# Output products in column tiles of two feature blocks by two token halves, in a float32 convolution and SwiGLU kernel

## The chip, the cores and the metric

The kernel runs on one core of a Trainium2 chip. A core has five engines that work side by side: TensorE (PE in the profile, its weight loads PEld), VectorE (DVE), ScalarE (ACT), GpSimd (POOL) and SyncE (SP), which here only issues DMAs. The metric is the device time of one execution in microseconds (us), less is better. Before the change it was 2796.47 us, the median of three runs (2788.88 to 2798.66).

## The reference

Two blocks follow each other: a causal convolution of 7 taps, whose taps differ by head, and a feed-forward block with a norm and a gated unit. Everything is float32.

```python
# x: (8, 4096, 192), weight: (8 heads, 7 taps)
w = softmax(weight, axis=-1)
x_pad = concatenate([zeros(8, 6, 192), x], axis=1)
x_unf = x_pad[:, arange(4096)[:, None] + arange(7)[None, :], :]   # seven shifted copies
y = einsum('hk,bskhg->bshg', w, x_unf).reshape(32768, 192)

rms = sqrt(mean(y * y, axis=-1, keepdims=True) + 1e-6)
xn = y / rms * rms_g
g, val = xn @ w_gate, xn @ w_val              # 192 -> 1536, twice
out = (silu(g) * val) @ w_out                 # 1536 -> 192
```

## The kernel before

The 32768 tokens are worked through in 32 pairs of token tiles, 2 x 512 tokens each. The first pair is computed plainly, by code of its own, beside the preparation of the weights. Each of the other 31 goes through two stages on TensorE, here called P and O:

- P, the up-projection. Both projections are computed as sums of 15 products for each of four groups of hidden features, in two halves of the array: 120 matmuls of 64 rows by 512 columns. They read `xb` (the normalised input, features by tokens) and `xc` (sums of parts of it, the "input sums").
- O, the output products. The product with `w_out` is done by seven products of half-size blocks (Strassen's scheme in Winograd's form), each over six chunks of 128 hidden features.

Each `yield` in a generator of matmuls is one step. A list, ORDER, tells how the steps and all other operations follow each other in a pair: `p2` is two steps of matmuls, `VX5` is input sum 5 on VectorE, `AS40.1.0` a copy on ScalarE, `GS3.1` a sum on GpSimd; a minus sign at the end means that the operation belongs to the pair before. Its beginning and its end:

```python
ORDER = (
    "p2 VT22- AS40.1.0 VT11- p2 AS40.0.0 Dload- Vbc- p2 AF0.0.0 VC.0.0 Dst1- AF0.1.0",
    ...
    "p1 Asq p2 GX1 GS4.5 p3 VC22 p2 GS4.4 p2 Vred p6 VC21 p2 VX5 p4 VX10 p3 VX9 VT21 p2",
    "Gpow p4 VT12 p3 GX4 p3",
)
```

The steps of a pair:

```python
def products(self):
    for u in self.units:                       # P: four groups of hidden features
        for v, i in CHAIN:                     # 15 products
            for h in range(2):                 # two halves of the array's rows
                u.product(h, v, i)             # 64 x 512 columns
                yield
    for form, b, lo, hi in OUTS:               # O: seven forms, 42 chunks in all
        first = form in (1, 7)
        if first:
            self.open(b, False)
        for k in range(lo, hi):
            cols = self.left(form, k).rearrange("p (b q e) -> p q b e", q=NQ, e=Q)
            for m in range(NM):                # NM = 3 blocks of Q = 32 output features
                for q in range(NQ):            # NQ = 4 quarters of the tokens
                    nc.tensor.matmul(
                        out=self.bank(b)[q * Q : (q + 1) * Q, m * P : (m + 1) * P],
                        lhsT=RIGHT[form][:, k, m, :], rhs=cols[:, q],
                        start=(first and k == 0 and m == 0), stop=True,
                        skip_group_check=True, tile_position=(0, q * Q),
                    )
                yield
```

The stationary operand is a block of the weights, 128 hidden features by 32 output features; it fills one column tile of the array, 32 of its 128 columns. The hidden values stream through it, 128 tokens in one matmul. Four such matmuls, one for each column tile, belong together.

The results stand in a PSUM bank with output features in the partitions and tokens along the columns. VectorE turns blocks of 32 x 32 into the output tile:

```python
def turn(self, src, g, n):
    if g not in self.o_sb:
        self.o_sb[g] = outs.tile([P, T // P, D], F32, name="o_sb")
    to = self.o_sb[g][:].rearrange("p b (m n e) -> p m n b e", n=2, e=Q)
    for m in range(NM):
        nc.vector.transpose(
            out=to[:, m, n],
            in_=src[:, m * P : (m + 1) * P].rearrange("p (b e) -> p b e", e=Q),
        )
```

During O the engines other than TensorE already work for later pairs: the convolution of the pair after next (`cv`, and `sq`, `red`, `pow` for the norm), and the input sums of the next pair (`X`), after its input has been fetched:

```python
def fetch(p):                                  # Dfetch: four DMAs of 384 KB
    xd = scr.pop(p)
    for g in (1, 0):
        for rows in (LOW, UPP):
            nc.sync.dma_start(
                out=xb[rows, g],
                in_=xd[:, g * T : (g + 1) * T].rearrange("(k p) t -> p k t", p=HP),
            )

def x_sum(i, eng="V"):                         # VX0 .. VX10, or GX
    d, a, b = XSUM[i]
    e = nc.gpsimd if eng == "G" else nc.vector
    e.tensor_tensor(out=xc[:, d, :], in0=x_op(a), in1=x_op(b), op=ALU.add)
```

`xb` and `xc` exist once, so the fetch waits for the last product of P that reads them.

Of the kernel before, what the change touches and what calls it, by code (L numbers as in the profile page):

```python
# [19 lines left out]
def kernel(  # L20
# [10 lines left out]
    nc = tc.nc  # L31
    P = nc.NUM_PARTITIONS
# [10 lines left out]
    T = 512  # L43
# [3 lines left out]
    HP = P // 2  # L47
    KP = D // HP
    Q = 32
    NQ = P // Q  # L50
# [7 lines left out]
    LOW, UPP = slice(0, HP), slice(HP, P)  # L58
# [29 lines left out]

    SPAN = 1509
    ORDER = (  # L90
        "p2 VT22- AS40.1.0 VT11- p2 AS40.0.0 Dload- Vbc- p2 AF0.0.0 VC.0.0 Dst1- AF0.1.0",
        "Dst0- p2 Gmul- p2 AS41.1.0 VC.1.0 AS41.0.0 p2 AS00.1.0 VS00.0.0 p2 GX7- VD5.0.0 p2",
        "VD5.1.0 AS42.0.0 VS42.1.0 p2 Dplace- VR1.0.0 AS51.1.0 AS51.0.0 p2 VR1.1.0 p2 AF2.0.0",
        "VR0.1.0 p1 VR0.0.0 AF2.1.0 p1 AF3.0.0 p1 VF3.1.0 AS44.0.0 p1 AS44.1.0 AG1.0.0",
        "VR5.0.0 p2 GM1.1.0 AG5.0.0 VR2.0.0 VR2.1.0 p2 VR3.1.0 AG4.0.0 p3 VR5.1.0 AS40.0.1 p1",
        "VR3.0.0 AS40.1.1 GM5.1.0 p1 VM4.1.0 AF0.0.1 AG3.0.0 p2 AF0.1.1 p1 VC.0.1 AG0.0.0 p1",
        "VC.1.1 GM3.1.0 p1 AS41.1.1 VS41.0.1 p1 GM0.1.0 GS3.0 VS00.0.1 p1 AS00.1.1 p2 VD5.0.1",
        "p1 VD5.1.1 p1 AS42.0.1 AS51.0.1 VS51.1.1 p1 GS1.0 VR1.0.1 AS42.1.1 p1 AG2.0.0 p1",
        "VR1.1.1 p1 VR0.0.1 p1 AF2.0.1 VR0.1.1 GM2.1.0 p1 AF2.1.1 p1 VF3.0.1 p1 AF3.1.1",
        "VS44.0.1 p1 AG0.0.1 GS3.1 p1 VR2.0.1 p1 GS2.0 AS44.1.1 AG1.0.1 p2 VR2.1.1 AG2.0.1",  # L100
        "GM1.1.1 p1 VR5.0.1 p1 AG4.0.1 VR5.1.1 p1 GM2.1.1 VM4.1.1 p1 AG5.0.1 AS40.0.2 p1",
        "VR3.0.1 VR3.1.1 p2 AS40.1.2 AF0.0.2 GM0.1.1 p1 AF0.1.2 VC.0.2 GS3.2 p1 VC.1.2 p1",
        "AS41.0.2 AS41.1.2 p1 GM5.1.1 p1 AS00.0.2 p2 GS1.2 VS00.1.2 p1 VD5.0.2 AS51.0.2 p1",
        "VD5.1.2 AS42.0.2 p1 AS51.1.2 p1 GS2.2 VS42.1.2 p1 AG3.0.1 VR1.0.2 p1 GM3.1.1 p1",
        "VR0.1.2 p1 AF2.0.2 VR0.0.2 p1 AF2.1.2 p1 AF3.0.2 p1 GS4.2 AS44.0.2 p1 VR1.1.2 p1",
        "GS1.1 VF3.1.2 AG0.0.2 p1 AS44.1.2 p1 VR5.0.2 VR2.0.2 p1 VR2.1.2 AG1.0.2 AG5.0.2 p1",
        "VR3.1.2 p1 GM1.1.2 AG4.0.2 VR5.1.2 AS40.0.3 p2 GM0.1.2 GM5.1.2 VR3.0.2 p1 AS40.1.3",
        "p1 VM4.1.2 p1 AF0.0.3 p1 AF0.1.3 AG3.0.2 p1 VC.0.3 p1 VC.1.3 p1 VS41.0.3 GM3.1.2",
        "AS41.1.3 AS00.0.3 p2 VS00.1.3 AG2.0.2 p1 GS3.3 GS1.3 p2 VD5.1.3 AS42.0.3 AS51.1.3",
        "VD5.0.3 VS42.1.3 p2 AS51.0.3 VR1.0.3 GS2.1 p1 GM2.1.2 p2 VR0.1.3 VR1.1.3 p1 GS2.3 p1",  # L110
        "AF2.0.3 AF2.1.3 p1 VR0.0.3 p1 VF3.1.3 p1 AF3.0.3 VS44.0.3 p1 AG1.0.3 p1 VS44.1.3",
        "AG0.0.3 VR5.0.3 p3 GM1.1.3 VR3.0.3 GS3.4 VR2.0.3 p1 GS4.3 Acv0_2 p1 VR3.1.3 p1",
        "Vcv1_2 p2 AG4.0.3 p1 AG3.0.3 p1 GM3.1.3 p1 Dfetch VM4.1.3 Acv0_1 p3 Acv0_0 p2",
        "AG2.0.3 p2 Vcv1_0 p1 VR5.1.3 p1 GS1.4 VR2.1.3 p1 Vcv1_1 p1 GS3.5 p1 Ac1 p1 AG5.0.3",
        "p4 Vcv2_2 p2 GS2.4 p6 Vcv2_0 p1 VM5.1.3 p3 Vcv2_1 As7 p2 Vcv3_2 p1 Vcv3_0 p1 GS1.5",
        "p4 Vcv3_1 p1 GS4.1 p1 Vcv4_0 p2 Vcv5_0 GS2.5 p3 GS4.0 Vcv4_2 p5 Vcv4_1 p1 Vcv5_2 p3",
        "GX0 Vcv5_1 p5 VX3 Ac2 Vcv6_2 p3 VX2 p7 VX8 p4 GM2.1.3 Vcv6_0 VX6 VM0.1.3 p9 Vcv6_1",
        "p1 Asq p2 GX1 GS4.5 p3 VC22 p2 GS4.4 p2 Vred p6 VC21 p2 VX5 p4 VX10 p3 VX9 VT21 p2",
        "Gpow p4 VT12 p3 GX4 p3",
    )  # L120

    cst = ctx.enter_context(tc.tile_pool(name="cst", bufs=1))
# [115 lines left out]
    def load_out(i):  # L238
# [28 lines left out]
        out=taps[:], in0=w_sb[:], in1=stat[:].to_broadcast([P, H, K]), op=ALU.subtract  # L267
# [7 lines left out]
        out=taps[:], in0=taps[:], in1=ssum[:].to_broadcast([P, H, K]), op=ALU.mult  # L275
# [403 lines left out]
    def put(at, do):  # L679
        heapq.heappush(line, (at, next(tick), do))  # L680
# [10 lines left out]
    def copy(eng, dst, src, s=1):  # L691
        if eng == "A":
            nc.scalar.activation(out=dst, in_=src, func=AF.Copy, scale=float(s))  # L693
        elif s < 0:
            nc.vector.tensor_scalar(out=dst, in0=src, scalar1=-1.0, scalar2=None, op0=ALU.mult)
        else:
            nc.vector.tensor_copy(out=dst, in_=src)
# [86 lines left out]
    NM = D // (2 * Q)  # L784
# [16 lines left out]
    RIGHT = {1: B11, 2: B21, 3: B22, 4: T4, 5: T1, 6: T2, 7: T3}  # L801

    class Pair:
# [35 lines left out]
        def products(self):  # L839
            for u in self.units:  # L840
                for v, i in CHAIN:
                    for h in range(2):
                        u.product(h, v, i)
                        yield
            for form, b, lo, hi in OUTS:
                first = form in (1, 7)
                if first:
                    self.open(b, False)
                for k in range(lo, hi):
                    cols = self.left(form, k).rearrange("p (b q e) -> p q b e", q=NQ, e=Q)  # L850
                    for m in range(NM):
                        for q in range(NQ):
                            nc.tensor.matmul(  # L853
                                out=self.bank(b)[q * Q : (q + 1) * Q, m * P : (m + 1) * P],
                                lhsT=RIGHT[form][:, k, m, :], rhs=cols[:, q],
                                start=(first and k == 0 and m == 0), stop=True,
                                skip_group_check=True, tile_position=(0, q * Q),
                            )
                        yield

        def some(self, b):
            return self.bank(b)[:, 0 : NM * P]
# [1 line left out]
        def turn(self, src, g, n):  # L864
            if g not in self.o_sb:
                self.o_sb[g] = outs.tile([P, T // P, D], F32, name="o_sb")
            to = self.o_sb[g][:].rearrange("p b (m n e) -> p m n b e", n=2, e=Q)
            for m in range(NM):
                nc.vector.transpose(  # L869
                    out=to[:, m, n],  # L870
                    in_=src[:, m * P : (m + 1) * P].rearrange("p (b e) -> p b e", e=Q),
                )

        def sum(self, form, k, eng):
# [9 lines left out]
        def do(self, eng, name):  # L884
            act, *at = name.split(".")
            p, n = self.p, NM * P
            if len(at) == 2:
                self.units[int(at[1])].do(eng, act, int(at[0]))
            elif at:
                self.sum(int(act[1]), int(at[0]), eng)  # L890
            elif act == "c1":
                self.open("Y", True)
                copy(eng, self.some("Y"), self.some("X"))
            elif act in ("s7", "c2"):
                t = self.tl[act] = tiles.pop(0)
                copy(eng, t[:, 0:n], self.some("Z" if act == "s7" else "X"))
            elif act in ("C22", "C21"):
                t = self.tl["s7" if act == "C22" else "c2"][:, 0:n]
                b = "X" if act == "C22" else "Z"
                nc.vector.tensor_tensor(out=t, in0=self.some(b), in1=t, op=ALU.add)  # L900
                if b == "Z":
                    self.close(b)
            elif act in ("T22", "T21"):
                t = self.tl.pop("s7" if act == "T22" else "c2")
                self.turn(t, 1, int(act[2]) - 1)
                tiles.append(t)
            elif act in ("T11", "T12"):
                b = "Y" if act == "T11" else "X"
                self.turn(self.bank(b), 0, int(act[2]) - 1)
                self.close(b)  # L910
            elif act in ("st0", "st1"):
                g = int(act[2])
                r = p * PT + g * T
                nc.sync.dma_start(
                    out=out[r : r + T, :].rearrange("(j p) d -> p j d", p=P), in_=self.o_sb.pop(g)[:]
                )
            else:
                self.ahead(eng, act)

# [16 lines left out]
    def plain(hts):  # L936
# [27 lines left out]
        def values():  # L964
            for u, g, f in groups:
# [7 lines left out]
                yield  # L973

        return products(), silus(), values()

    LAG = 138
# [116 lines left out]
    p, sl, v = plain(hts)  # L1094
# [31 lines left out]
    c = base + 200  # L1126
# [60 lines left out]
```

## Time and profile before

| | before |
|---|---|
| time, median of three runs | 2796.47 us |
| span of the profiled run | 2787.9 us |
| PE busy, matmul records | 2650.6 us, 39418 |
| DVE busy, instructions | 2400.9 us, 3914 |
| ACT busy, instructions | 1505.7 us, 2778 |
| POOL busy, instructions | 2078.4 us, 1695 |
| mean granted TensorE clock | 0.989 |
| DMA queue q1: packets, MB | 444240, 133.44 |

A line of the profile that describes a group of instructions names the line of the program, the engine, the operation, output and inputs, the shape and the count; behind the bar stand the time in which the group was busy, the mean of one in ns, and the idle time of the engine just before. The timeline has the start and the length in us, then the instructions that it merges; in brackets stands idle time before them, and what ended it. A table of stretches has for each engine its busy time and the number of instructions, then the granted clock, the DMA engines' share and the rate. "issue" is time in which an engine waited for nothing that the profile shows. Each float32 matmul of the program stands as two records in the trace. SP's entries are the issuing of DMAs, not their transfers.

The program's lines that matter: L732 is the product of P, L853 that of O, L655 an input sum, L445 a tap of the convolution, L869 a transpose into the output tile, L646 the fetch of the next pair's input, L882 a sum of hidden values on GpSimd, L693 a copy on ScalarE and L697 one on VectorE.

### The profile page before, as it was taken

The numbers are of one execution on the slowest core, as the hardware profiler recorded it, in microseconds if no ns is written. First come the engines' busy times: TensorE is split into PE (matmuls) and PEld (weight loads), VectorE is DVE, ScalarE is ACT, GpSimd is POOL, SyncE is SP. The second block draws the span as 40 slices with busy tenths as digits, with TensorE's granted clock in tenths as the row PEclk, the third lists the DMA queues.
The fourth block names the chain that finished last, engine by engine and source line by source line (L and its number), as shares of the span: only waits on it lengthen the run. The fifth ranks groups of instructions, "written<-read, shape, count | busy, mean of one in ns | idle before, by whom it ended". The sixth has DMA issues, their size and how long they took to land.

```text
span 2787.9 us, 91977 instructions
## 1 busy us (share of the span) xinstructions
PE 2650.6 (95%) x39418; PEld 1826.5 (66%) x39418; DVE 2400.9 (86%) x3914; ACT 1505.7 (54%) x2778; POOL 2078.4 (75%) x1695
## 2 busy tenths in 40 slices
PE   6999999999999999999999999999999999999999
PEld 3766667666677566676666666666766666666666
DVE  8898888988888988888888888888988888888876
ACT  5266544565445665446655456544566544565444
POOL 3987777777768777677777777777877777877767
PEclk9999999999999999999999999999999999999999
DMA  6311332131231213322223213223212233121210
GB/s 135 65 41 37 60 60 49 35 59 37 60 60 30 54 37 60 60 37 47 45 52 60 56 29 58 38 60 60 41 44 49 47 60 60 25 58 37 47 36 14
DMA packets 445209, 139.34 MB, mean 50 GB/s; under 512 B 385024, under 2 KB 419328, under 8 KB 444673
## 3 DMA queue, kind: packets, MB, share of 16 engines
q1 hardware_dynamic: 444240, 133.44, 24.1%
q8 instruction: 308, 5.05, 0.8%
q14 instruction: 101, 0.83, 0.1%
q10 hardware_dynamic: 560, 0.03, 0.0%
HBM read 83.87 MB, written 49.55 MB: 48 GB/s over the span
## 4 chain that ended last, share of the span: by engine, by line
PE 77%; DVE 9%; issue 6%; POOL 3%; ACT 2%; DMA 1%; SPq 1%; POOLq 0%; DVEq 0%
PE ps L732 56%; PE ps L853 19%; DVE xc L655 3%; DVE ps L445 1%; POOL ht L882 1%; PE ps L990 1%; DVE ht L756 1%; ACT ps L437 1%; PE ps L950 1%; DMA xh<-in_x_dram 1%; POOL nt L882 1%; DVE y L445 1%; DVE s L471 1%; DVE o_sb L869 1%; POOL xc L655 1%
## 5 line engine op out<-in xcount | busy, mean ns | idle before, releaser
L732 PE MATMUL ps<-xc,wf 64*128 64x512 f32 x4960 | 1287.0, 595 | 6.1 <-DVE o_sb L869 4.9
L732 PEld LDWEIGHTS ps<-xc,wf 64*128 64x128 f32 x4960 | 630.0, 186 | 486.2 <-issue 359.6
L732 PE MATMUL ps<-xb,wf 64*128 64x512 f32 x2480 | 739.0, 589 | 0.0
L776 POOL TENSOR_TENSOR ht<-ht,tile 128x512 f32<-128x512 f32 x330 | 418.7, 1276 | 196.0 <-ACT tile L769 177.2
L693 ACT ACTIVATE tile<-ps 128x512 f32<-128x512 f32 (+1 forms) x634 | 360.5, 593 | 348.0 <-PE ps L732 185.8
L693 ACT ACTIVATE tls<-ps 128x512 f32<-128x512 f32 (+1 forms) x513 | 293.0, 588 | 437.5 <-PE ps L853 253.1
L732 PEld LDWEIGHTS ps<-xb,wf 64*128 64x128 f32 x2480 | 329.4, 187 | 252.3 <-issue 240.9
L693 ACT ACTIVATE ps<-ps 128x512 f32<-128x512 f32 (+1 forms) x651 | 358.9, 580 | 141.5 <-PE ps L732 90.4
L776 POOL TENSOR_TENSOR ht<-ht,tls 128x512 f32<-128x512 f32 x228 | 290.5, 1277 | 113.9 <-ACT tls L769 103.5
L882 POOL TENSOR_TENSOR early<-ht 128x512 f32<-128x512 f32 x279 | 354.7, 1276 | 9.7
L853 PE MATMUL ps<-ht,wo_sb 128*32 128x128 f32 x10416 | 338.4, 280 | 14.1 <-issue 13.0
L853 PEld LDWEIGHTS ps<-ht,wo_sb 128*32 128x32 f32 x10416 | 305.7, 113 | 47.5 <-POOL ht L776 23.5
L445 DVE SCALAR_TENSOR_TENSOR ps<-xh,tp,ps 128x512 f32<-128x512 f32 x435 | 299.8, 750 | 16.7 <-ACT ps L437 15.6
L853 PE MATMUL ps<-early,x 128*32 128x128 f32 x6696 | 220.4, 281 | 77.7 <-issue 77.6
L756 DVE TENSOR_TENSOR tile<-ps,tile 128x512 f32<-128x512 f32 x371 | 250.8, 684 | 25.3 <-ACT tile L693 21.8
L882 POOL TENSOR_TENSOR ht<-ht 128x512 f32<-128x512 f32 x186 | 238.2, 1281 | 30.1 <-DVE ht L776 20.4
L853 PE MATMUL ps<-ht,x 128*32 128x128 f32 x8928 | 258.7, 273 | 1.6 <-issue 1.0
L853 PEld LDWEIGHTS ps<-early,x 128*32 128x32 f32 x6696 | 199.0, 113 | 88.1 <-issue 87.0
L853 PEld LDWEIGHTS ps<-ht,x 128*32 128x32 f32 x8928 | 247.1, 110 | 8.1 <-issue 7.8
L769 ACT ACTIVATE tile<-tile 128x512 f32<-128x512 f32 x371 | 230.3, 628 | 0.0
L756 DVE TENSOR_TENSOR ht<-ps,tile 128x512 f32<-128x512 f32 x333 | 222.9, 684 | 4.6
L756 DVE TENSOR_TENSOR ht<-ps,tls 128x512 f32<-128x512 f32 x287 | 194.3, 683 | 2.3
(128 smaller groups left out, 3346.7 us busy)
## 6 DMA issues: line engine op xcount, KB each, us to landing
xb<-xd SPq DMA_DIRECT2D x124, 384.0 KB
out_dram<-o_sb SPq DMA_DIRECT2D x64, 384.0 KB
xd<-yn SPq DMA_DIRECT2D x248, 96.0 KB
xh<-in_x_dram SPq DMA_DIRECT2D x192, 105.0 KB
xh<-in_x_dram SPq DMA_DIRECT2D x56, 98.4 KB
ht<-in_moe_w_gate_dram SPq DMA_DIRECT2D x12, 192.0 KB
ht<-in_moe_w_val_dram SPq DMA_DIRECT2D x12, 192.0 KB
tls<-in_moe_w_out_dram SPq DMA_DIRECT2D x8, 192.0 KB
```

The source lines that it names most:

```text
L437: nc.scalar.mul(bank(*acc[p, j])[:], xk, w)
L445: nc.vector.scalar_tensor_tensor(out=dst, in0=xk, scalar=w, in1=at, op0=ALU.mult, op1=ALU.add)
L471: nc.vector.tensor_reduce(out=ss[:], in_=sq, axis=AX.X, op=ALU.add)
L655: e.tensor_tensor(out=xc[:, d, :], in0=x_op(a), in1=x_op(b), op=ALU.add)
L693: nc.scalar.activation(out=dst, in_=src, func=AF.Copy, scale=float(s))
L732: nc.tensor.matmul(out=self.new(v, h, True) if first else self.old(v, h), lhsT=wf[self.u][HALF[h], WAT[i], :], rhs=x_op(XOP[i])[HALF[h]], ...
L756: nc.vector.tensor_tensor(out=self.hv(v) if h else t[:], in0=self.old(v, h), in1=t[:], op=plus(s))
L769: nc.scalar.activation(out=t[:], in_=src[:], func=AF.Silu)
L776: engine[eng].tensor_tensor(out=self.hv(v), in0=src, in1=t[:], op=ALU.mult)
L853: nc.tensor.matmul(out=self.bank(b)[q * Q : (q + 1) * Q, m * P : (m + 1) * P], lhsT=RIGHT[form][:, k, m, :], rhs=cols[:, q], start=(first ...
L869: nc.vector.transpose(out=to[:, m, n], in_=src[:, m * P : (m + 1) * P].rearrange("p (b e) -> p b e", e=Q),)
L882: engine[eng].tensor_tensor(out=dst, in0=a, in1=b, op=op)
```

## The change

A step of O had three rounds of four matmuls with 128 columns each, one round for a block of 32 output features, one matmul for each quarter of the tokens. Now the four column tiles hold two blocks of output features by two halves of the tokens, and 256 columns stream in one matmul; the third block still goes in four quarters of 128 columns. So there are eight matmuls in a chunk and not twelve. The purpose is fewer instructions on TensorE for the same products.

The results then lie in another pattern in the PSUM bank. The transposes take 256 and 128 columns, two where there were three, and the output tile is stored by three DMAs, each with runs of 64 features (256 bytes), where one DMA had stored rows of 192 features (768 bytes). The list ORDER was searched anew; it has 204 steps and not 246, and gives some operations to other engines.

```diff
@@ ORDER (29 rows, all replaced; the first, the last two)
-        "p2 VT22- AS40.1.0 VT11- p2 AS40.0.0 Dload- Vbc- p2 AF0.0.0 VC.0.0 Dst1- AF0.1.0",
+        "p2 VT21- p2 AS40.1.0 VT11- GX4- AS40.0.0 p2 Vbc- AF0.0.0 Gmul- AF0.1.0 p2 Dst1-",
 ...
-        "p1 Asq p2 GX1 GS4.5 p3 VC22 p2 GS4.4 p2 Vred p6 VC21 p2 VX5 p4 VX10 p3 VX9 VT21 p2",
-        "Gpow p4 VT12 p3 GX4 p3",
+        "p2 VX9 p1 Dload p1 VX3 p2 VC22 p2 VX6 p2 GS4.4 Vred p3 GS4.5 p4 VX5 p2 VX2 p1 VX7 p2",
+        "VX10 p2 Gpow VT12 p2 VT22 p2 VC21 p1",
@@ products
                 for k in range(lo, hi):
-                    cols = self.left(form, k).rearrange("p (b q e) -> p q b e", q=NQ, e=Q)
-                    for m in range(NM):
-                        for q in range(NQ):
-                            nc.tensor.matmul(
-                                out=self.bank(b)[q * Q : (q + 1) * Q, m * P : (m + 1) * P],
-                                lhsT=RIGHT[form][:, k, m, :], rhs=cols[:, q],
-                                start=(first and k == 0 and m == 0), stop=True,
-                                skip_group_check=True, tile_position=(0, q * Q),
-                            )
-                        yield
+                    src, right = self.left(form, k), RIGHT[form][:, k]
+                    fresh = first and k == 0
+                    wide = src.rearrange("p (b q e) -> p q b e", q=2, e=Q)
+                    slim = src.rearrange("p (b q e) -> p q b e", q=NQ, e=Q)
+                    for i in range(NQ):
+                        self.tile(b, i, 0, 2 * P, right[:, i // 2], wide[:, i % 2], fresh)
+                    yield
+                    for i in range(NQ):
+                        self.tile(b, i, 2 * P, P, right[:, 2], slim[:, i], False)
+                    yield
+
+        def tile(self, b, i, at, n, left, cols, fresh):
+            nc.tensor.matmul(
+                out=self.bank(b)[i * Q : (i + 1) * Q, at : at + n], lhsT=left, rhs=cols,
+                start=fresh, stop=True, skip_group_check=True, tile_position=(0, i * Q),
+            )
@@ turn
-            to = self.o_sb[g][:].rearrange("p b (m n e) -> p m n b e", n=2, e=Q)
-            for m in range(NM):
+            to = self.o_sb[g][:].rearrange("p a d -> p (a d)").rearrange(
+                "p (b n e) -> p n b e", n=2, e=Q
+            )
+            for lo, hi in ((0, 8), (8, 12)):
                 nc.vector.transpose(
-                    out=to[:, m, n],
-                    in_=src[:, m * P : (m + 1) * P].rearrange("p (b e) -> p b e", e=Q),
+                    out=to[:, n, lo:hi],
+                    in_=src[:, lo * Q : hi * Q].rearrange("p (b e) -> p b e", e=Q),
                 )
@@ do: st0, st1
-                nc.sync.dma_start(
-                    out=out[r : r + T, :].rearrange("(j p) d -> p j d", p=P), in_=self.o_sb.pop(g)[:]
-                )
+                o = self.o_sb.pop(g)[:].rearrange("p a d -> p (a d)")
+                o = o.rearrange("p (b d) -> p b d", d=HP)
+                for c, rows, lo, hi in ((0, LOW, 0, 8), (1, UPP, 0, 8), (2, slice(0, P), 8, 12)):
+                    n = T // (hi - lo)
+                    to = out[r : r + T, c * HP : (c + 1) * HP].rearrange("(b p) d -> p b d", p=n)
+                    nc.sync.dma_start(out=to, in_=o[rows, lo:hi, :])
```

## The prediction

> **What bounds the kernel now.** I read the page first, then the table of busy time by stage, then the timeline and the waits of TensorE (PE) in one stage, then VectorE's (DVE) timeline in the same stage. The page:
>
> ```profile
> span 2787.9 us, 91977 instructions
> PE 2650.6 (95%) x39418; PEld 1826.5 (66%) x39418; DVE 2400.9 (86%) x3914; ACT 1505.7 (54%) x2778; POOL 2078.4 (75%) x1695
> ...
> q8 instruction: 308, 5.05, 0.8%
> ...
> PE 77%; DVE 9%; issue 6%; POOL 3%; ACT 2%; DMA 1%; SPq 1%; POOLq 0%; DVEq 0%
> ```
>
> PE is the bound: busy 95%, and 77% of the chain of waits. The share to notice is "issue 6%": time in which PE waited for nothing that the profile shows, some 167 us. The stages tell where it lies. Every pair of token tiles after the first has a P stage (up-projection products, L732) and an O stage (output products, L853). Two pairs in sequence, P, O, P, O:
>
> ```profile
> core 0: us, PE busy (x) PEld busy (x) DVE busy (x) ACT busy (x) POOL busy (x), PEclk, DMA share, GB/s
> 1594.17:1646.73 52.56, 52.56 (x241) 28.35 (x241) 46.46 (x80) 40.08 (x76) 41.71 (x34) 1.00 0.16 36
> 1646.73:1681.35 34.62, 30.90 (x1010) 29.79 (x1009) 27.89 (x46) 6.75 (x11) 22.63 (x20) 0.90 0.38 70
> 1681.35:1733.91 52.56, 52.56 (x244) 28.40 (x241) 46.19 (x79) 40.08 (x76) 41.28 (x33) 1.00 0.14 34
> 1733.91:1765.93 32.02, 28.78 (x1009) 27.28 (x1008) 28.50 (x44) 6.75 (x11) 22.83 (x20) 1.00 0.42 72
> ```
>
> P is the same to the hundredth, 52.56 us, PE busy throughout. O varies (34.62, 32.02), and its granted clock fell to 0.90 in one of them. From the second pair's P (starts at 227.18 in the timeline) to the last pair's (2701.94) there are 29 pairs, so a pair takes 85.34 us and a mean O stage 85.34 - 52.56 = 32.78 us. Now PE inside the long O stage:
>
> ```profile
> 1646.73 4.14 PE L853 MATMUL ps<-ht,wo_sb 128*32 128x128 f32 x144
> 1650.68 3.66 PE L853 MATMUL ps<-early,x 128*32 128x128 f32 x123
> 1658.06 1.28 PE L853 MATMUL ps<-early,x 128*32 128x128 f32 x19 [3.72 <-issue]
> ```
>
> The first 144 matmuls start within 3.95 us: 27.4 ns each. All 1008 at that pitch would take 27.65 us. In the trace four start within 17 ns, one in each column tile, and the next four 109 ns later. Then PE stands still for 3.72 us, on "issue". The waits of PE over the whole run say the same:
>
> ```profile
> PE ps L853 <- issue: 96.4, 61, 4.2
> ...
> PE ps L732 <- DVE o_sb L869: 4.9, 10, 0.8
> ```
>
> PE hardly ever waits for another engine's result. What does it wait for? The instruction queue moved 308 packets and 5.05 MB, 16.4 KB each: at 64 bytes, 256 instructions, or 128 pairs of weight load and matmul. Spacings fit: without a stall, its packets start 3.5 us apart in O stages, which is 128 x 27.4 ns. In the stall above the packet starts at 1655.56 and takes 1.16 us; matmuls resume at 1658.06. And SyncE shows what else was in the DMA engines:
>
> ```profile
> 1646.38 3.26 SPq L646 DMA_DIRECT2D xb<-xd  x4
> ```
>
> The next pair's input (1.5 MB, 2 KB packets) is fetched as soon as P has read the old one, that is in the first 8 us of every O stage, where the stalls of 1.4 to 4.4 us are. Later crossings of a block cost 0.3 to 1.2 us. So an O stage is 27.65 us of streaming and 5.13 us of starving for instructions.
>
> [...]After the stall of 3.72 us the groups of four start 214 ns apart for some 3 us, and the stage's clock is 0.90[...]
>
> **The change, part by part.**
>
> *Matmuls.* An O stage has 42 steps (seven forms, six chunks each). Before: 12 tile products a step, each 128 columns; after: four of 256 and four of 128. Columns a tile: 3 x 128 = 384 before, 256 + 128 = 384 after. Nothing is saved in streaming. Two records a product: 42 x 12 x 2 = 1008 before, 42 x 8 x 2 = 672 after. A narrow group keeps 109.7 ns (3.95 us / 36), a wide one should take twice that less one fixed part, 217 ns: 84 x (217 + 109.7) = 27.4 us, against 27.65. The direct gain is 0.2 us.
>
> *Instruction stream.* An instruction pair lasts 40.8 ns on average, (217 + 109.7)/8, instead of 27.4, so a block lasts 128 x 40.8 = 5.2 us instead of 3.5. A block that is asked for when another is used up must arrive within that. Later in O it now arrives about 3.8 us after the request (3.5 and the usual stall of 0.3), at most 4.7: below 5.2, so those stalls go. While the input is fetched it takes 3.5 + 1.4 to 3.5 + 4.4 = 4.9 to 7.9 us, typically 6.4: about 1.2 us of stall is left, and rarely enough to halve the clock. PE alone would give O = 27.4 + 1.2 = **28.6 us**.
>
> *Evacuation.* Each turn into the output tile needs two transposes (256 and 128 wide) instead of three of 128; the data are the same, 12 become 8 a pair at 0.28 us busy each. I count 0.1 us a stage.
>
> *Stores.* Three DMAs a half in runs of 256 bytes instead of one in runs of 768: 3072 packets a pair instead of 1024. They are issued early in P, where the DMA share is 0.15 and PE uses instructions slowly (480 of them in 52 us). I count nothing, beyond more DMA busy time.
>
> *New order.* Counting the list: six PSUM copies go from VectorE to ScalarE (net with one fork the other way: ScalarE 86 to 91 entries, VectorE 112 to 110, GpSimd 48 to 45), and two input sums go from GpSimd to VectorE. In P, VectorE had 46.2 us of 52.56 and gets lighter: six copies at a pitch of 0.6 us less, one fork and one multiply more, about 43.8 us. ScalarE at 40 + 3 us stays off the path. In O it gets heavier, and that is the sum to watch. Busy 27.9 and 28.5 us before, say 28.0; two more input sums at their mean of 1.11 us (245.7 us over 221) add 2.2; one result add of 0.6 that now falls into P goes: 29.6 us. The next P's second product needs the last input sum, after which only three of these operations stand (a sum and two turns, 1.75 us). VectorE's own waits in O are some 1.4 us (0.55 for the first convolution copy, 0.9 for the square). The last sum is ready 29.6 - 1.75 + 1.4 = **29.2 us** after O begins.
>
> ```profile
> 1667.20 1.75 DVE L655 TENSOR_TENSOR xc<-xb,xc 128x512 f32<-128x512 f32 x1 [5.05 <-POOL xc L655]
> ...
> 1679.13 0.69 DVE L655 TENSOR_TENSOR xc<-xb 128x512 f32<-128x512 f32 x1
> ```
>
> In the long stage VectorE idled 5.05 us, behind GpSimd, which waited for the starved PE, and still finished its last sum (1679.13 + 0.69) 1.5 us before the next P. Its slack was PE's starving; take that away and the two engines come level.
>
> *Sum.* The stalls of PE and VectorE's work lie beside each other, so O is the larger: 29.2 us instead of 32.78. P stays at 52.56. 31 O stages x 3.6 = 111 us; 2796.5 - 111 = **2685 us**, 4% less.
>
> **Rivals.**
>
> (a) Instruction fetch is fully hidden and VectorE keeps up: O = 27.4, gain 5.4 x 31 = 167 us, 2630 us. For: blocks of 5.2 us. Against: the 1.5 MB of input still land in the same 8 us, and VectorE's 29 us.
>
> (b) VectorE becomes the bound for the pair: it was busy 46.2 + 28 = 74 of 85 us and would be at 73 of 81. If its waits of about 11 us a pair only shift instead of vanishing, a pair takes 84 us and the gain is 40 us: 2755 us. For: an in-order engine at 90%. Against: most of its largest wait (POOL, 93.2 us in all) hung on the starved PE, and the order was searched for this stage length.
>
> (c) The fetch latency, not the count, sets the stall: a crossing during the input fetch costs the same, but there are 5.25 blocks an O stage instead of 7.9. The gain is then a third of 5.13 us plus the clock: about 1.8 x 31 = 56 us, 2740 us.
>
> (d) Narrow stores hold up something: 2048 more packets a pair. Against: output buffers are needed again a whole pair later. A few microseconds at most.
>
> **Range and chances.** 2685 lies between (a) and (c)/(b). PE cannot stream faster, so below 2640 is very unlikely; above 2745 needs (b) in full. Range 2650 to 2745. Faster by over 2% means below 2740.5, an O and P stage together under 83.5 us: 0.84. Within 2%: 0.13. Slower would need a new wait of over 5 us a pair: 0.03.
>
> **What would show it.** Right: L853 with a third fewer records and groups 217 and 109 ns apart; the instruction queue at about 5.05 - 31 x 672 x 64 bytes = 3.7 MB; issue waits of L853 cut from 96 to some 30 us, all in the first 8 us of O; P still 52.56; PEclk 1.00 in O stages; O near 29; PE waiting now and then at the start of P for an input sum. Wrong: P stages longer than 52.6 (a bank or sum comes late, rival b), or issue gaps as long as before (rival c), or wide groups well over 217 ns.

## The result, and the profile after

The changed kernel takes **2669.88 us** (median of four runs, 2668.73 to 2672.97), against 2793.55 us for the kernel before on the same chip: a ratio of 0.956, 95% interval 0.954 to 0.958. The forecast was 2685 us.

In the changed kernel L862 is the product of O and L877 the transpose. L908 is a "chunk sum": VectorE adds a PSUM bank, in which PE has added up several forms of O, to a tile in SBUF. A chunk, 128 hidden features of one form, takes twelve matmuls before and eight after; an O stage has 42 chunks (what the prediction and the text on the change call its steps).

From the page after:

```profile
span 2668.9 us, 71301 instructions
PE 2605.1 (98%) x29002; PEld 1761.3 (66%) x29002; DVE 2346.1 (88%) x3726; ACT 1582.4 (59%) x2933; POOL 1980.1 (74%) x1604
...
q8 instruction: 227, 3.72, 0.6%
...
PE 85%; DVE 8%; POOL 2%; issue 2%; SPq 1%; DMA 1%; ACT 0%; DVEq 0%; POOLq 0%
```

PE has 10416 matmul records fewer (31 x 336) and is busy 98% of a shorter span. The instruction queue went from 5.05 to 3.72 MB, as worked out. All its packets are of 16384 bytes: 308 for PE's 78980 instructions in the trace before (weight loads, matmuls, 144 others), 227 for 58148 after, so 256 instructions of 64 bytes in a packet, a block. "issue" on the chain of waits fell from 6% to 2%. The busy time by stage, P, O, P, O:

```profile
core 0: us, PE busy (x) PEld busy (x) DVE busy (x) ACT busy (x) POOL busy (x), PEclk, DMA share, GB/s
1578.13:1607.77 29.64, 27.83 (x673) 24.87 (x672) 29.25 (x44) 6.58 (x11) 23.53 (x20) 1.00 0.50 85
1607.77:1660.26 52.49, 52.49 (x242) 29.89 (x240) 44.21 (x74) 42.69 (x81) 37.86 (x30) 1.00 0.15 31
1660.26:1688.25 27.99, 27.65 (x674) 20.48 (x673) 27.64 (x42) 6.58 (x11) 22.43 (x20) 1.00 0.53 90
1688.25:1741.17 52.92, 52.92 (x245) 32.58 (x241) 44.84 (x76) 42.77 (x81) 38.54 (x30) 1.00 0.14 31
```

There are two kinds of pair now. After a long O (29.64) P takes 52.49 us; after a short one (27.99), where VectorE was busy for 27.64 us of it, P takes 52.92. PE in the long O, on the timeline:

```profile
1578.13 4.11 PE L862 MATMUL ps<-ht,wo_sb 128*32 128x256 f32 x96
1582.05 4.08 PE L862 MATMUL ps<-early,x 128*32 128x256 f32 x96
1585.95 1.46 PE L862 MATMUL ps<-ht,wo_sb 128*32 128x256 f32 x27
1589.22 0.96 PE L862 MATMUL ps<-ht,wo_sb 128*32 128x128 f32 x19 [1.81 <-issue]
```

The first 96 records start within 3.92 us, 40.8 ns each. One stall on issue remains, 1.81 us, in the place where the 3.72 us stood. The waits of PE over the run:

```profile
PE ps L862 <- issue: 21.0, 19, 2.4
...
PE ps L862 <- DVE tile L908: 2.7, 8, 0.4
```

96.4 us of waiting for instructions became 21.0, and waits for VectorE (L908) appear. From the second pair's P (223.66) to the last pair's (2581.58) a pair takes 81.31 us: 4.03 less than before, and 29 x 4.03 = 116.9 of the 119.0 us by which the span shrank.

The 75 us of waits are not all of the gain: the clock is a part too. The kernel before, in the long O stage that the prediction looks at, up to the stall, in it, and after it:

```profile
1648.00:1654.34 6.34, 6.34 (x231) 6.07 (x219) 5.79 (x10) 3.01 (x6) 5.57 (x6) 1.00 0.98 226
1654.34:1658.06 3.72, 0.00 (x2) 0.01 (x2) 3.69 (x6) 0.00 (x0) 1.25 (x1) 0.88 0.18 36
1658.06:1663.90 5.84, 5.84 (x112) 5.26 (x116) 4.09 (x7) 0.49 (x1) 1.69 (x2) 0.50 0.01 3
```

The DMA engines are full (0.98) while the input comes in. By the trace's DMA packets the last of the input ends at 1655.58, and the instruction packet starts just then, at 1655.56. Then PE runs for 5.8 us at half the clock, its groups of four 214 ns apart. In 11 of 30 O stages before, the granted clock is 0.90 to 0.95, and each of the 11 has a wait on issue of 2.65 us or more; in the changed kernel the longest is 2.4 us, and no O stage is below 1.00. By the spacing of the groups I estimate that the slow clock cost the kernel before some 21 us.

### The profile page after: what moved, and what is told of

Read it like the earlier page. It is cut to its first block, busy times and chain, and to the rows that moved or that the text cites. A ratio compares the mean times of both kernels' runs of the same rounds, so it can differ in the third digit from the quotient of the medians.

```text
span 2668.9 us, 71301 instructions
## 1 busy us (share of the span) xinstructions
PE 2605.1 (98%) x29002; PEld 1761.3 (66%) x29002; DVE 2346.1 (88%) x3726; ACT 1582.4 (59%) x2933; POOL 1980.1 (74%) x1604
## 3 DMA queue, kind: packets, MB, share of 16 engines
q8 instruction: 227, 3.72, 0.6%
## 4 chain that ended last, share of the span: by engine, by line
PE 85%; DVE 8%; POOL 2%; issue 2%; SPq 1%; DMA 1%; ACT 0%; DVEq 0%; POOLq 0%
PE ps L732 60%; PE ps L862 24%; DVE ps L445 3%; DVE xc L655 2%; PE ps L961 1%; DVE ht L756 1%; POOL wf L350 1%; DVE y L445 1%; DVE ht L776 0%; POOL nt L890 0%; SPq L218 0%; POOL ht L890 0%; DMA ht<-in_moe_w_val_dram 0%; SPq L1099 0%; DMA x<-in_x_dram 0%
## 5 line engine op out<-in xcount | busy, mean ns | idle before, releaser
L732 PEld LDWEIGHTS ps<-xc,wf 64*128 64x128 f32 x4960 | 685.1, 186 | 435.4 <-issue 269.8
L693 ACT ACTIVATE tile<-ps 128x512 f32<-128x512 f32 (+1 forms) x744 | 421.5, 592 | 419.2 <-PE ps L732 238.5
L776 POOL TENSOR_TENSOR ht<-ht,tile 128x512 f32<-128x512 f32 x291 | 369.5, 1276 | 235.0 <-ACT tile L769 232.7
L693 ACT ACTIVATE ps<-ps 128x512 f32<-128x512 f32 x620 | 338.1, 581 | 72.1 <-PE ps L732 69.5
L862 PE MATMUL ps<-ht,wo_sb 128*32 128x256 f32 (+1 forms) x6944 | 316.9, 326 | 19.0 <-issue 15.6
L862 PEld LDWEIGHTS ps<-ht,wo_sb 128*32 128x32 f32 x6944 | 232.0, 110 | 104.7 <-issue 25.2
L862 PE MATMUL ps<-ht,x 128*32 128x128 f32 (+1 forms) x5952 | 251.5, 326 | 0.0
L862 PEld LDWEIGHTS ps<-ht,x 128*32 128x32 f32 x5952 | 221.0, 110 | 24.8
L756 DVE TENSOR_TENSOR tls<-ps,tls 128x512 f32<-128x512 f32 x276 | 187.5, 684 | 32.8 <-PE ps L732 19.2
L862 PE MATMUL ps<-early,x 128*32 128x256 f32 (+1 forms) x4464 | 198.9, 326 | 5.5 <-issue 5.5
L769 ACT ACTIVATE tls<-tls 128x512 f32<-128x512 f32 x276 | 172.5, 625 | 25.5 <-DVE tls L756 25.5
```

Source lines behind the costliest of these rows:

```text
L732: nc.tensor.matmul(out=self.new(v, h, True) if first else self.old(v, h), lhsT=wf[self.u][HALF[h], WAT[i], :], rhs=x_op(XOP[i])[HALF[h]], ...
L756: nc.vector.tensor_tensor(out=self.hv(v) if h else t[:], in0=self.old(v, h), in1=t[:], op=plus(s))
L769: nc.scalar.activation(out=t[:], in_=src[:], func=AF.Silu)
L776: engine[eng].tensor_tensor(out=self.hv(v), in0=src, in1=t[:], op=ALU.mult)
L862: nc.tensor.matmul(out=self.bank(b)[i * Q : (i + 1) * Q, at : at + n], lhsT=left, rhs=cols, start=fresh, stop=True, skip_group_check=True, ...
```

## The experiments

The theory: TensorE starved because its instruction packets stand in line behind the next pair's input, and the change cures this by asking for fewer of them. The rivals: the new order of the other engines brings the gain; or PE can't be fed at that pitch at all. In the table, "pair", "O" and "P" are means from the trace's start times, O to the next P's start; O takes in the first pair and the other two don't, so they don't quite add up. Ratios are against the kernel before on the same chip, with 95% intervals. Where there is one run only, no ratio stands.

| kernel | us | ratio | pair | O | P |
|---|---|---|---|---|---|
| before | 2793.55 | 1 | 85.34 | 32.74 | 52.57 |
| changed | 2669.88 | 0.956 (0.954 to 0.958) | 81.31 | 28.59 | 52.69 |
| changed, wide matmuls split | 2807.34 | 1.008 (1.005 to 1.011) | 85.67 | 33.17 | 52.51 |
| changed, old order | 2681.58 | 0.963 (0.960 to 0.966) | 81.69 | 29.12 | 52.56 |
| before, no input fetch | 2674.18 | one run | 81.42 | 28.86 | 52.56 |
| changed, no input fetch | 2660.57 | one run | 80.92 | 27.99 | 52.92 |
| before, fetch halves swapped | 2721.63 | 0.977 (0.974 to 0.980) | 83.04 | 30.43 | 52.56 |
| changed, fetch halves swapped | 2660.02 | 0.956 (0.955 to 0.958) | 80.92 | 27.98 | 52.93 |
| six matmuls a chunk | 2662.67 | 0.957 (0.956 to 0.959) | 80.96 | 28.06 | 52.88 |
| six, one sum moved | 2654.54 | 0.954 (0.953 to 0.956) | 80.63 | 28.06 | 52.57 |
| no fetch, two sums fewer | 2648.88 | one run | 80.52 | 28.01 | 52.51 |
| swapped, one sum moved, C22 earlier | 2652.76 | 0.952 (0.950 to 0.954) | 80.65 | 27.47 | 53.16 |

**Only the number of instructions undone.** All else of the change stays.

```diff
-    self.tile(b, i, 0, 2 * P, right[:, i // 2], wide[:, i % 2], fresh)
+    for s in range(2):
+        part = wide[:, i % 2, s * 4 : (s + 1) * 4]
+        self.tile(b, i, s * P, P, right[:, i // 2], part, fresh and s == 0)
```

> The changed kernel with each 256-column matmul cut into two of 128 columns; layout, transposes, stores and the new order stay. Theory (instruction stream): 1008 records an O stage again, the stalls on issue come back, O about 32.5 us, time 2770 to 2800 us. Rival (the new order or the transposes bring the gain): stays at 2670 to 2690 us, O about 28.6 us.

Measured: 2807.34 us, slower even than before by 0.8%. PE's waits and its timeline in one O stage:

```profile
PE ps L864 <- issue: 95.6, 63, 4.1
```

```profile
1483.85 4.21 PE L864 MATMUL ps<-ht,wo_sb 128*32 128x128 f32 x144
1487.80 1.97 PE L864 MATMUL ps<-early,x 128*32 128x128 f32 x63
1491.70 2.46 PE L864 MATMUL ps<-early,x 128*32 128x128 f32 x81 [1.93 <-issue]
```

The stalls are back at the size of before (96.4 us), with new order, transposes and stores in place. So the gain hangs on the number of instructions (the page after has 29002 weight loads for 29002 matmul records). Why this kernel is a little slower than before (pairs of 85.67 against 85.34 us) these runs don't tell.

**Only the order undone.** The new tiling under the old list; the wide matmuls take two of the list's steps, so that a chunk has three as before.

```diff
     for i in range(NQ):
         self.tile(b, i, 0, 2 * P, right[:, i // 2], wide[:, i % 2], fresh)
-    yield
+        if i % 2:
+            yield
```

> The changed kernel's matmuls, transposes and stores under the old order (three steps a chunk, so that the old list fits). Theory (instruction stream): most of the gain stays, O 28.6 to 30 us, time 2675 to 2715 us; what is lost against 2670 us is VectorE and GpSimd coming late in the shorter stage. Rival (the order brings the gain): 2740 us or more, with waits for VectorE or GpSimd at TensorE.

Measured: 2681.58 us, ratio 0.963. The old order keeps the gain but for about 12 us: O is 29.12 us instead of 28.59. Waits on issue are 16.6 us in this run; what comes instead are waits of PE for VectorE's transposes at the start of P (15.2 us, 24 times), as expected.

**The input fetch taken away,** from the kernel before and from the changed one. All pairs after the first compute with an old input, so their times only serve as a measurement.

```diff
-    fetch(p + 1) if act == "fetch" else x_sum(int(act[1:]), eng)
+    act == "fetch" or x_sum(int(act[1:]), eng)
```

> The kernel before, without the fetch of the next pair's input in O (leaves out 1.5 MB of DMA a pair; all later pairs compute with an old input). Theory (instruction packets queue behind the input): the stalls of 1.4 to 4.4 us in the first 8 us go, those of 0.3 us at the crossings of blocks stay, granted clock near 1.00, O 29 to 30 us, time 2690 to 2730 us. Rival (PE cannot be fed at that pitch whatever the DMA engines do): stalls as before, over 2770 us.

> The changed kernel, without the fetch of the next pair's input in O (leaves out the same DMA). Theory: no stall on issue is left, every pair like the undisturbed ones of the changed kernel, 28.0 + 53.0 = 81.0 us where the mean is 81.3: time about 2660 us, 0.4% less. If the fetch stalls were all that is left beside streaming: 27.5 + 52.5 = 80.0 us a pair, 2630 us.

Measured: before without the fetch 2674.18 us, within 0.2% of the changed kernel's time, with 1008 records an O stage. Two consecutive stages of it, and its waits:

```profile
1448.05:1500.60 52.55, 52.55 (x240) 28.22 (x240) 46.45 (x80) 40.02 (x76) 41.56 (x33) 1.00 0.15 35
1500.60:1529.46 28.86, 28.12 (x1009) 27.56 (x1008) 27.11 (x44) 6.74 (x11) 22.87 (x20) 1.00 0.17 24
```

```profile
PE ps L732 <- DVE o_sb L869: 12.1, 22, 0.8
...
PE ps L853 <- issue: 3.7, 8, 0.8
```

Waiting on issue fell from 96.4 to 3.7 us: without the input PE is fed its 1008 records in an O of 28.86 us, 1.21 us over the 27.65 of streaming at 27.4 ns each. What is left are waits for VectorE. It beat the expectation of 2690 to 2730 us, which had kept the small stalls at later blocks; they went too. The changed kernel without the fetch is faster by only 0.39 us a pair, 80.92 against 81.31, and its O and P are those of its undisturbed pairs. That is what the theory said (about 2660 us; 2660.57 measured), and not the 2630 us of a kernel that is held up by the fetch alone.

So the collision, with the slow clock that follows it, costs 85.34 - 81.42 = 3.92 us a pair with the old tiling and 0.39 with the new. The difference, 3.53 us, is most of the 4.03 that the change brings; the other 0.50 us shows between the two kernels without a fetch (81.42 against 80.92). The new order, the two transposes and the wider matmuls all lie in it, and no run separates them.

**The fetch in another order.** The half of the tokens whose last product comes six products before the end of P is fetched first.

```diff
-        for g in (1, 0):
+        for g in (0, 1):
             for rows in (LOW, UPP):
```

> The changed kernel, the next input fetched in the other order: first the token half whose last product comes six products before the end of P (some 2.6 us earlier), so that part of the 1.5 MB lands before O begins. Theory (instruction packets queue behind the input): shorter stalls in the first 12 us of O, 0.4 us a stage instead of 0.8, most pairs then at the 81.0 us of the undisturbed ones: 2660 to 2668 us, at most 0.4% under the changed kernel. Rival (the stalls depend on the number of bytes alone): 2670 us.

> The changed kernel with the fetch's token halves in the other order, beside the changed kernel on the same chip. Theory: 0.3 to 0.5% under the changed kernel (a pair of 80.9 us instead of 81.3), 2655 to 2662 us.

> The kernel before, with nothing changed but the order of the fetch's token halves. Theory (stalls come from instruction packets behind 1.5 MB of input): with half of the input landing before O begins, the stalls of the first 12 us shrink, but a block of instructions still lasts only 3.5 us: 2680 to 2730 us. If the whole 1.5 MB matters and not its place: 2780 us.

SyncE's timeline, first of the changed kernel, where this O begins at 1660.26:

```profile
1660.28 2.58 SPq L646 DMA_DIRECT2D xb<-xd  x4
```

then of the swapped one, where O begins at 1572.79:

```profile
1567.17 6.87 SPq L646 DMA_DIRECT2D xb<-xd  x4
```

The first two of the four DMAs now go out 5.6 us before P ends, earlier than I had reckoned, and the others at its end. In the trace the input's data are through 5.5 us after O begins (mean of the O stages), where they took until 9.5 us, and the DMA engines' share of a short O stage is 0.38 and not 0.53. With the new tiling the stalls are gone: 80.92 us a pair, the same as without any fetch. Beside the changed kernel on one chip (2670.61 us, ratio 0.958, interval 0.956 to 0.961) it took 2661.29 us (0.955, 0.953 to 0.958): 0.35% less by the medians, more than the spread of either, though the intervals of the two ratios overlap. With the old tiling the swap alone brings 2.3%. From the waits of PE in that kernel:

```profile
PE ps L853 <- issue: 45.8, 61, 2.1
```

Half of the waiting on issue is left there, with blocks of 3.5 us (128 x 27.4 ns); with blocks of 5.2 us (128 x 40.8 ns) the same fetch leaves none in the list of PE's waits. The longest wait is 2.1 us now, and the mean granted clock 0.998 where it was 0.989.

**Still fewer instructions.** Three column tiles take the three feature blocks and stream 384 tokens; the fourth streams the last 128 tokens for each block in turn. 504 records instead of 672; the output goes in six stores a half, an edit that isn't shown.

```diff
-    for i in range(NQ):
-        self.tile(b, i, 0, 2 * P, right[:, i // 2], wide[:, i % 2], fresh)
+    for i in range(NM):
+        self.tile(b, i, 0, 3 * P, right[:, i], src[:, 0 : 3 * P], fresh)
     yield
-    for i in range(NQ):
-        self.tile(b, i, 2 * P, P, right[:, 2], slim[:, i], False)
+    for m in range(NM):
+        self.tile(b, 3, m * P, P, right[:, m], src[:, 3 * P :], fresh and m == 0)
     yield
```

> The changed kernel with six matmuls a chunk instead of eight: three column tiles hold the three feature blocks and stream 384 tokens, the fourth streams the last 128 tokens for each block; six stores a half. 504 records an O stage. Theory: a block of instructions lasts 7.0 us, so hardly a stall on issue is left; streaming stays 27.5 us if the four column tiles run on independently, and VectorE sets the pair at 81.0 us: about 2660 us. If a tile's successive matmuls hold back the others (issue in order), O grows by up to a third, 36 us, and the time goes above 2800 us.

Measured: 2662.67 us. One O stage of it:

```profile
1410.72:1438.78 28.06, 27.85 (x505) 27.41 (x504) 27.70 (x42) 6.60 (x11) 22.48 (x20) 1.00 0.51 89
```

The stalls are gone. The four column tiles run on side by side although one of them gets three matmuls for the others' one: by the start times a chunk takes 0.645 us, against 0.650 with eight matmuls. VectorE (27.70 of 28.06 us) sets the stage. Fewer instructions and an earlier fetch end at the same 80.9 to 81.0 us.

**VectorE as the second bound.** In the changed kernel's short O stage, VectorE's timeline:

```profile
1677.07 1.68 DVE L655 TENSOR_TENSOR xc<-xb,xc 128x512 f32<-128x512 f32 x1
1678.67 2.97 DVE L655 TENSOR_TENSOR xc<-xb 128x512 f32<-128x512 f32 x3
1681.57 0.54 DVE L908 TENSOR_TENSOR tile<-ps,tile 128x384 f32<-128x384 f32 x1
...
1686.64 0.68 DVE L655 TENSOR_TENSOR xc<-xc 128x512 f32<-128x512 f32 x1
...
1688.33 0.51 DVE L908 TENSOR_TENSOR tls<-ps,tls 128x384 f32<-128x384 f32 x1
```

Between them stands no gap over 0.04 us. The first chunk sum, C22 in the list (1681.57), must read its PSUM bank before PE adds the next form to it, and PE stood until 1682.26; the second, C21 (1688.33 to 1688.84), releases the bank that P's second matmul takes, and that matmul's weights were loaded at 1688.89:

```profile
1682.26 1.51 PE L862 MATMUL ps<-ht,wo_sb 128*32 128x256 f32 x32 [0.34 <-DVE tile L908]
```

```profile
1688.89 0.72 PEld L732 LDWEIGHTS ps<-xc,wf 64*128 64x128 f32 x5 [0.35 <-DVE tls L908]
```

By the start times those are 0.3 to 0.7 us and 0.4 us a pair. First two of the nine input sums (2 and 7) were left out, with the fetch, to lighten VectorE:

> The changed kernel without the input fetch in O and without two of VectorE's nine input sums (leaves out both). Theory (with the stalls gone, VectorE's work in O holds TensorE back by 0.4 us at the chunk sums and 0.4 us at the start of P): both waits go, a pair falls from 80.9 to 80.0 to 80.2 us, time 2630 to 2640 us. Rival (those waits are the order of the instructions or PSUM banks, not VectorE's load): stays at 2660 us.

Measured: 2648.88 us, half of what was expected. P fell to 52.51, its wait went; O stayed at 28.01. Both sums stand behind C22 in the order, so C22 came no earlier. VectorE's load set the wait at the start of P; for the one in O its order is left, which the last run tests.

Then input sum 7, which P needs only for its twelfth product, was moved to GpSimd, on the six-matmul kernel:

```diff
-    ... "VX2 p1 VX7 p2",          # VectorE, in O
+    ... "VX2 p1 p2",
-    "... VT11- GX4- AS40.0.0 ..."
+    "... VT11- GX4- GX7- AS40.0.0 ..."   # GpSimd, at the start of P
```

> Six matmuls a chunk, and one input sum that is needed late (the twelfth product of P) moved from VectorE in O to GpSimd at the start of P. If six matmuls stream as fast as eight, theory: VectorE's load in O falls by 0.65 us, a pair takes 80.3 to 80.6 us: 2640 to 2650 us, ratio to the kernel before about 0.945 to 0.95. If GpSimd's sum comes too late for P or delays its norm scaling, no gain over the six matmuls alone.

Measured: 2654.54 us, 80.63 us a pair: P is back at 52.57, O unchanged at 28.06. That is just outside what was expected (80.3 to 80.6 us a pair, 2640 to 2650 us); C22 had kept its place. Last, all three on eight matmuls: the swapped fetch, the moved sum, and C22 ahead of input sum 3.

```diff
-    "... p1 Dload p1 VX3 p2 VC22 p2 VX6 ..."
+    "... p1 Dload p2 VC22 VX3 p1 p2 VX6 ..."
```

> The changed kernel as it is, as a control on the same chip: 2660 to 2672 us, ratio to the kernel before 0.953 to 0.959.

> The fetch in the other order, input sum 7 moved to GpSimd at the start of P, and the chunk sum C22 placed before input sum 3 on VectorE. Theory: no stall on issue, neither of the two waits for VectorE: O 27.6, P 52.5, a pair 80.1 us: 2632 to 2642 us, ratio to the kernel before 0.944 to 0.949. If the wait at the chunk sums is not the sum's place behind input sum 3, it stays 0.5 us a pair and the time is about 2650 us.

Measured: **2652.76 us**, ratio 0.952 (0.950 to 0.954), beside 2670.61 for the changed kernel on the same chip: 0.7% less. This kernel and the six-matmul one with the moved sum (0.953 to 0.956) are the fastest of those that leave nothing out; their intervals overlap. Its stages O and P, and PE's weight loads at the start of a P:

```profile
1406.40:1433.84 27.44, 27.44 (x674) 20.02 (x673) 27.02 (x40) 6.58 (x11) 21.80 (x17) 1.00 0.39 64
1433.84:1487.02 53.18, 53.18 (x245) 30.62 (x241) 44.99 (x77) 42.73 (x81) 40.31 (x34) 1.00 0.21 45
```

```profile
1354.06 0.31 PEld L732 LDWEIGHTS ps<-xc,wf 64*128 64x128 f32 x4 [0.55 <-DVE tile L908]
```

O has no wait left, 27.44 us is streaming. The swapped fetch alone had left O at 27.98 and the moved sum alone (with six matmuls) at 28.06, so it was C22's place that held PE. But P grew to 53.18: PE arrives sooner at the second chunk sum, which VectorE does after two turns. I had expected that wait to go as well (80.1 us a pair; 80.65 measured). To put that sum ahead of the two turns is the next step; it wasn't tried.

## Why the prediction held, step by step

- **Streaming.** Forecast 27.4 us, with 217 + 109.7 = 326.7 ns for a wide and a narrow group. On the timeline after, 32 records (four of each group) start every 1.30 us, 325 ns; by the start times a wide group takes 216 ns and a narrow one 109 (medians of 1660 and 1621 whole groups), so a wide one is 2 ns less than two narrow ones; 84 x 325 = 27.3 us, against 27.65 before. Right: the direct gain is small.
- **Instruction stream.** Right in its mechanism: the split kernel and the ones without a fetch show that it is the instructions and that they wait behind the input. That a block must come within the time of the one before it shows in the trace before, too. All 55 gaps of over 0.5 us between PE's matmuls in O end at the same place, 193 or 194 instructions past a multiple of 256, the edge of a block. Of the 308 packets none starts sooner than 47 instructions before PE is at the edge one block ahead, and none later than 255 after that edge, when PE stands at the next one. From a packet's start to PE's going on it takes 2.2 to 3.1 us. The forecast was 1.2 us of stall an O stage and some 30 us of waits on issue, none late in O; measured are 0.8 us (by the start times) and 21.0 us. That the mean O of 28.59 us meets "PE alone", 28.6, is luck: 27.4 + 0.8 is 28.2, and most of the rest is the wait at C22, which the forecast didn't have. Three readings were off. The stalls don't lie in the first 8 us of O: the one shown ran from 7.6 to 11.3 us after O began, and with the new tiling they end 8 to 12 us after it, since the input's data move until some 9.5 us. "5.13 us of starving" held too much: without the fetch 28.86 - 27.65 = 1.21 us stay, mostly waits for VectorE. And "later in O it now arrives about 3.8 us after the request" isn't borne out: without the fetch the stalls at later blocks vanish. Why they come with the fetch stays open. For the new tiling the term didn't matter; in the run of before without a fetch it made my expectation at least 16 us too high.
- **VectorE in O.** Forecast: the last input sum ready at 29.2 us, and therefore O = 29.2. This is the step that was mis-sized. In the O from 1660.26 the last sum ends at 1686.64 + 0.68, 27.1 us after O began. Nine sums take 8.0 us here, 0.89 each and not 1.11 (0.95 over the run). They overlap less with GpSimd: a sum takes 0.68 us while GpSimd is idle, which was so for 8 of 221 before and for 81 of 281 after, and 1.06 on average beside a busy GpSimd after. VectorE's own gaps are 0.35 us and not 1.4. These two make 3 us; 0.8 us of it is taken back because only 0.9 us of the work behind the last sum lies within O, not 1.75. "The larger of the two" came true stage by stage: the stall sets the long O stages, VectorE the short ones. The time came out 15 us lower: 0.61 us in O times 31 is 19, less 0.13 us a pair by which P is longer than forecast.
- **The start of P.** "PE waiting now and then at the start of P" came true, 0.4 us after each short O, though for a PSUM bank that a chunk sum frees and not for an input sum. With it a sign of being wrong came true as well, in a small way: P is longer than 52.6 us, 52.69 in the mean and 52.92 after a short O.
- **Stores and clock.** P shows no wait for the stores. The mean clock rose from 0.989 to 0.998; no O stage is below 1.00. The prediction's reading of the clock before was rough: half the clock lasted 5.8 us after the stall shown, not "some 3 us". And the length of a wait alone doesn't tell whether the clock falls: waits on issue of 2.65 and 2.74 us were followed by a lower clock, and four of 3.13 to 3.34 us were not.
- **Rivals.** (a), everything hidden, 2630 us: no, VectorE holds a pair at 80.9. (b), VectorE as the bound at 84 us a pair: no, at 81. (c), each crossing costs the same as before: no, the stall in the fetch's window fell from 3.1 us an O stage to 0.8 (gaps added up from the trace's start times, first 13 us of O), far more than by a third.

## What to carry to other kernels

When an engine waits on "issue", look at the instruction queue's packets beside the largest transfer that is under way. Here fewer and longer instructions helped: with the input fetched in O, blocks of 3.5 us left 96.4 us of waits in a run, blocks of 5.2 us 21.0. Before rewriting, look at when that transfer starts: exchanging two numbers in the fetch of the kernel before brought half of this change's gain by itself (2.3% against 4.4%). And once the starving is gone, look at the engine that it had given slack, here VectorE, busy for 27.64 us of a short O of 27.99: at what it does in which order as well as at how much.

## What the runs showed of the hardware that was not expected

- Instruction packets are delayed by data of the program's own DMAs: with 1.5 MB of input in each O stage PE waited 96.4 us on issue in a run of the kernel before, without it 3.7 us. In the stall shown the packet starts at 1655.56, the input having ended at 1655.58.
- In 15 of 30 O stages before, later blocks come some 0.2 us late as well (29 of them from 11 to 25 us after O begins), when the input's data are long through; without the fetch the waits on issue are 3.7 us in all. Why is open.
- After some waits on issue, from 2.65 us up in the kernel before, the granted clock fell (to 0.50 for 5.8 us of PE's work in the stage shown); in the changed kernel, with waits of up to 2.4 us, it fell in no O stage.
- Column tiles with unequal numbers of matmuls run on independently: three tiles with one matmul of 384 columns beside one with three of 128 take 0.645 us a chunk, eight equally shared matmuls 0.650.
